# Linear attention and a switched feed-forward on one core: first expert weights behind batch 1, gate weights cast later, paired copies grouped by bank

## The chip, the cores and the metric

The kernel runs on one core of a Trainium2 chip. The metric is the device time of one execution in microseconds (us). Before the change three runs gave 202.13, 200.18 and 201.58 us; the median is 201.58.

## The reference

```python
q_s = softmax(q, axis=-1)            # over the 64 elements of a head
k_s = softmax(k, axis=2)             # over the 576 positions
kv  = einsum('bhsd,bhse->bhde', k_s, v)
x   = (q_s @ kv) -> rows (8*576, 8*64) = (4608, 512)
logits = x @ w_gate + modality_bias[modality_id]
e = argmax(logits); gate = softmax(logits)[e]
out[row] = gate * (relu(x[row] @ w1[e]) @ w2[e])
```

There are 8 batches, 8 heads, 576 positions, 64 elements a head, 8 experts of 512 x 1024 x 512. Everything comes and goes as float32.

## The kernel before, in words

A row's modality is one of two, and its bias makes one expert likely for all rows of that modality. So the kernel finds two experts, A and B, from the bias alone, loads only their weights, and sorts the rows by modality: rows of A fill the buffer `xs` from the left, rows of B from the right. At the end it counts the rows whose true argmax is the assumed expert, checks that each pass read rows that were already in place, and repeats the work for all experts if a check fails (this does not happen with these inputs).

**Attention, batch by batch (0 to 7).** SyncE (SP) loads q, k and v; batches 0 and 1 come in two halves each of 576 KB, later ones whole. ScalarE takes exp of q in place (line 855) and of k into `ek` (888); a cast of v into `vb` (898) is on ScalarE for batches 0 and 1 and on GpSimd or ScalarE later. VectorE sums q (861), inverts (872, 873), and the normalised q goes to `eq` (877): on VectorE for batches 0 to 2, on GpSimd after. TensorE forms k^T v (990, two times 18 matmuls, one for each half of the heads), VectorE scales it into a block-diagonal `kvbd` (1017 to 1026). TensorE sorts q by a permutation matrix `perm` (1066), which is evicted to `et` (1078, 1080), and multiplies by `kvbd` (1105). Each result bank holds two chunks of 64 rows, and each chunk is copied twice into `xs` (1136), to side A and to side B at an offset read from a register (1040). In batches 0 and 1 ScalarE makes the copies of side A and VectorE those of side B; later batches have one engine for both.

**Feed-forward.** Side A and side B have nine passes of 256 rows each, and one more block of 128 rows in the middle has a path of its own. A pass is 16 matmuls for its two logits (1174; 8 for each 128 rows), 32 of 256 columns with W1 (1241), evictions `hT` (1208, 1210), and 16 of 512 columns with W2 (1254), scaled by the gate (1214, 1216) and scattered by GpSimd (1219).

**Order.** Nothing is scheduled at run time. A planner (class `Plan`) gets for each step the engines it may run on with assumed durations, a rank, what it depends on, and the buffers it takes; it plays the program through and writes the instructions in the order of its start times, each engine in one fixed queue. Where the planner sees TensorE idle before a time `quiet` it puts in matmuls that nobody reads (1498). The order of the transfers is the list `transfers` (line 391): numbers are batches, "a1" is the first weight matrix of expert A, "a2" its second, likewise for B. SP issues the batches; GpSimd issues the weights, which are cast on the way (534, 545). `w_awaits` holds a weight issue until the first tensor of the batch ahead of it has landed, and `ahead_of` holds a batch until the weights ahead of it have.

```python
transfers = [0, "a1", 1, "a2", 2, "b1", "b2", *range(3, B)]
l_wg = pl.op({"DMA": (0.4, 3.5)}, load_wg, rank=0)
wg_c = pl.op(
    on_dve(32), lambda _: nc.vector.tensor_copy(out=wg_sb, in_=wg_f), [l_wg, c_dve2], rank=11
)
```

The gate weights `wg_f` (466) are loaded behind batch 0 and cast to bf16 (526).

Of the kernel before, what the change touches and what calls it, by code (L numbers as in the profile page):

```python
# [15 lines left out]
ALU = mybir.AluOpType  # L16
ACT = mybir.ActivationFunctionType
# [202 lines left out]
def on_act(n):  # L220
    return {"ACT": (0.065 + n / 1200, 0.27 + n / 1200)}


def on_dve(n, rate=1, port=False):
    return {"DVE": (0.065 + n / 960 / rate, 0.28 + n / 960 / rate, port)}
# [17 lines left out]
def kernel(  # L243
# [12 lines left out]
    nc = tc.nc  # L256
    B, H, S, Dh = q.shape
# [5 lines left out]
    NJ = S // 64  # L263
# [21 lines left out]
    pl = Plan()  # L285
# [102 lines left out]

    issued = {}

    transfers = [0, "a1", 1, "a2", 2, "b1", "b2", *range(3, B)]

    ahead_of, w_awaits = {}, {}
    for i, x in enumerate(transfers):
# [82 lines left out]
    ahead = next(i for i, x in enumerate(transfers) if isinstance(x, str))  # L477
    for b in transfers[:ahead]:
        load_batch(b)
    l_wg = pl.op({"DMA": (0.4, 3.5)}, load_wg, rank=0)  # L480


    key = sb([P, 2], FP32, "key")
# [24 lines left out]
    def experts(_):  # L508
# [16 lines left out]
    wg_c = pl.op(  # L525
        on_dve(32), lambda _: nc.vector.tensor_copy(out=wg_sb, in_=wg_f), [l_wg, c_dve2], rank=11
    )
# [299 lines left out]
    final, edge, scaled_q = [], {}, []  # L827
# [7 lines left out]
        )  # L835

    started = {"a": False, "b": False}
    filled, perms = {}, []

    copier = [("ACT", "DVE")] * 2 + [(e, e) for e in ("DVE", "ACT", "ACT", "DVE", "ACT", "ACT")]  # L840

    def attention(b):
# [3 lines left out]
        R = 10.0 * b  # L846
# [79 lines left out]
        for (h, n), e in zip(halves, eqx):  # L926
# [5 lines left out]
                    rank=R + 1,  # L932
# [4 lines left out]
        for h, n in halves:  # L937
# [5 lines left out]
                    rank=R + 2,  # L943
# [5 lines left out]
        nq = []  # L949
        for j0, n in groups:  # L950
            n_ = n * HG * Dh
            ncost = on_pool(n_, 1.88)
            if b <= 2:
                ncost = on_dve(n_, 1, True)
            nq.append(
                pl.op(
                    ncost,
                    norm_q(j0, n),
                    [iq] + nq[:1],
                    rank=R + 1,  # L960
                    takes=[] if nq else [eqb],
                    uses=[eqb, qib, bq] if nq else [qib, bq],
                )
            )
# [7 lines left out]
        cv = []  # L972
        for hp in range(2):
# [5 lines left out]
                    rank=R + 0.5,  # L979
# [21 lines left out]
        for hp in range(2):  # L1001
# [5 lines left out]
                    rank=R + 2,  # L1007
# [25 lines left out]
        o_ki = pl.op({"DVE": (0.45, 0.55)}, kinv_run, kvo, rank=R + 2, takes=[kib], uses=kvp)  # L1033
        o_kb = pl.op({"DVE": (1.24, 1.4)}, kvbd_run, [o_ki, c_pool2], rank=R + 2, takes=[kvb], uses=[*kvp, kib])

        ets, win, firsts = [], [], []
        av = {}

        def load_off(e):
# [8 lines left out]

        los = [
            pl.op(  # L1050
                {e: (1.2 if e == "ACT" else 0.6, 1.3)},
                load_off,
                [o_off] + filled.get(b - 2, [])[-2:],
                rank=R + (2.2 if b == 1 else 0.2),
            )
            for e in dict.fromkeys(copier[b])
        ]
        for gi, (j0, nj) in enumerate(groups):
            sbuf = Buf(r_ps)
            w = nj * 64  # L1060

            def s1(_, j0=j0, nj=nj, sbuf=sbuf):
                t = ps_t[sbuf.idx]
                for jj in range(nj):
                    for hp in range(2):
                        nc.tensor.matmul(  # L1066
                            out=view(t, [[2 * nj * 64, 2], [1, 64]], hp * nj * 64 + jj * 64),
                            lhsT=eq[eqb.idx][:, j0 + jj, P * hp : P * hp + P],
                            rhs=perm[pmb.idx][:, j0 + jj, :],
                            start=True,  # L1070
                            stop=True,
                        )

            def ev(e, j0=j0, nj=nj, sbuf=sbuf):
                dst = view(et[etb.idx], [[S, KD], [1, nj * 64]], j0 * 64)
                src = view(ps_t[sbuf.idx], [[nj * 64, KD], [1, nj * 64]])
                if e == "ACT":
                    nc.scalar.copy(out=dst, in_=src)  # L1078
                else:
                    nc.vector.tensor_copy(out=dst, in_=src)  # L1080

            o1 = pl.op(
                on_pe(*[P] * (2 * nj)),
                s1,
                [nq[gi], o_pm] + firsts,
                rank=R + 3,
                takes=[sbuf] if gi else [sbuf, etb],
                uses=[eqb, pmb],
                lag=lag,
            )  # L1090
            firsts = firsts or [o1]
            o2 = pl.op(
                {**on_act(KD * w), **on_dve(KD * w)},
                ev,
                [o1],
                rank=R + 3,
                uses=[sbuf, etb],
            )
            ets.append(o2)
        for gi, (j0, nj) in enumerate(groups):  # L1100
            xbuf = Buf(r_ps)

            def s2(_, j0=j0, nj=nj, xbuf=xbuf):
                for c in range(KD):
                    nc.tensor.matmul(  # L1105
                        out=view(ps_t[xbuf.idx], [[1, nj * 64]], c * nj * 64),
                        lhsT=kvbd[kvb.idx][:, c, :],
                        rhs=et[etb.idx][:, c, j0 * 64 : (j0 + nj) * 64],
                        start=True,
                        stop=True,  # L1110
                    )

            o3 = pl.op(
                on_pe(*[nj * 64] * KD),
                s2,
                [ets[gi], o_kb],
                rank=R + 4,
                takes=[xbuf],
                uses=[kvb, etb],
                lag=lag,  # L1120
            )
            for jj in range(nj):
                for side in range(2):

                    def put(e, jj=jj, j0=j0, nj=nj, side=side, xbuf=xbuf):
                        c = b * NJ + j0 + jj
                        a = av[e][(j0 + jj) // 2]
                        if j0 + jj < NJ - 1:
                            a = a >> 16 if jj else a & 0xFFFF
                        a = nc.s_assert_within(a, 0, 64 * c, skip_runtime_bounds_check_because=WHY)  # L1130
                        if side:
                            a = a + (N - 64 - 64 * c)
                        p = next(x for x in (passes_b if side else passes_a) if x[0] >= b)
                        dst = window(a, p, 64)
                        src = view(ps_t[xbuf.idx], [[nj * 64, KD], [1, 64]], jj * 64)
                        w_ = nc.scalar.copy(out=dst, in_=src) if e == "ACT" else nc.vector.tensor_copy(out=dst, in_=src)  # L1136
                        if b >= 3 and not started["ab"[side]]:
                            started["ab"[side]] = True
                            for before in id_ins:
                                sync(w_, before, "windows overlap the digits of places")  # L1140
                        if not j0 + jj and b:
                            sync(w_, edge[side], "windows of the batch before reach into this one's")
                        if j0 + jj == NJ - 1:
                            edge[side] = w_
                        if b == B - 1:
                            final.append(w_)

                    before = win[-2] if len(win) > 1 else filled[b - 1][side - 2] if b else None

                    across = win[-1 - 2 * side] if j0 + jj == NJ - 1 else None  # L1150
                    same = before and before.costs.keys() == {copier[b][side]}
                    win.append(
                        pl.op(
                            on_dve(256) if copier[b][side] == "DVE" else on_act(256),
                            put,
                            [o3, o_id if b >= 3 else None, *los, None if same else before, across],
                            rank=R + 4,
                            uses=[xbuf],
                        )
                    )  # L1160
                    if same:
                        pl.follow(win[-1], before)
        filled[b] = win


    L = sb([P, NSL, E], FP32, "L")
# [324 lines left out]
        gs = [ffn(side, *p, rank=2.0 * i + side) for side, p in enumerate((pa, pb))]  # L1491
    ffn_rest(gs, 2.0 * i + 0.7)

    quiet = 32.0

    def unread(_):

# [11 lines left out]
    cnt = sb([P, 1], FP32, "cnt")  # L1509
# [22 lines left out]
    for i, (n, need) in enumerate(early):  # L1532
        so_far = aoff[0:1, NJ * (n + 1) : NJ * (n + 1) + 1]
        o_ = 1 + 2 * i
        nc.vector.tensor_scalar(
            out=ok[:, o_ : o_ + 1], in0=so_far, scalar1=float(need), scalar2=None, op0=ALU.is_ge
        )
        nc.vector.tensor_scalar(
            out=ok[:, o_ + 1 : o_ + 2],
            in0=so_far,  # L1540
            scalar1=float(S * (n + 1) - need),
            scalar2=None,
            op0=ALU.is_le,
        )
    okm = sb([1, 1], FP32, "okm")
    nc.vector.tensor_reduce(out=okm, in_=ok, op=ALU.min, axis=AX.X)
    nrest = sb([1, 1], I32, "nrest")
# [108 lines left out]
```

## Time and profile before

| what | value |
|---|---|
| runs | 202.13, 200.18, 201.58 us |
| profiled execution | 200.07 us, span 198.4 us |
| TensorE busy | 181.1 us, 91% of the span |
| VectorE / ScalarE / GpSimd busy | 152.3 / 124.5 / 94.8 us |
| granted TensorE clock, mean | 0.987 |
| unread matmuls of line 1498 | 57, 15.3 us |

The profiled execution's 200.07 us are its span and 1.67 us around it. Spans of TensorE are modelled where matmuls are pipelined, so a busy TensorE is not one at its peak; a clock of 1.00 is 2.4 GHz, 0.50 is 1.2 GHz.

### The profile page before, as it was taken

How to read it: one execution, taken by the hardware profiler on the slowest of the kernel's cores; microseconds unless marked ns; L12 is line 12 of the kernel's file. 1: busy time of each engine (PE TensorE's matmuls, PEld its weight loads, DVE VectorE, ACT ScalarE, POOL GpSimd, SP SyncE). 2: the span in 40 equal slices, each digit the busy share in tenths (PEclk: the TensorE clock that was granted, in tenths of full speed). 3: DMA queues.
4: the chain of work that ended last, by engine and by line, in shares of the span. 5: the costliest groups of instructions: out<-in, count | busy, mean ns of one | idle time of the engine just before them, and what ended most of it. 6: DMA issues, size and time to landing. Idle time of an engine off the chain costs nothing.

```text
span 198.4 us, 5000 instructions
## 1 busy us (share of the span) xinstructions
PE 181.1 (91%) x1757; PEld 123.9 (62%) x1757; DVE 152.3 (77%) x406; ACT 124.5 (63%) x246; POOL 94.8 (48%) x119
## 2 busy tenths in 40 slices
PE   0979986789999999999999999999899999999970
PEld 0435474457596666758685867586757756766740
DVE  3879998789999997958878999856788656655750
ACT  2765889679494786999998996699898000000000
POOL 7089303944540369598496329893112311331241
PEclk9999999699999999999999999999999999999998
DMA  5999999999999999998979941120202102211202
GB/s 189 355 280 259 390 294 247 397 287 211 212 336 407 399 389 340 295 377 267 386 288 280 398 165 55 56 109 0 109 0 107 76 33 106 106 56 53 96 32 90
DMA packets 18588, 42.33 MB, mean 213 GB/s; under 512 B 1913, under 2 KB 1913, under 8 KB 18562
## 3 DMA queue, kind: packets, MB, share of 16 engines
q1 hardware_dynamic: 13344, 28.33, 40.2%
q0 software_dynamic: 5200, 13.64, 23.8%
q8 instruction: 14, 0.23, 0.4%
q14 instruction: 12, 0.10, 0.1%
q10 hardware_dynamic: 18, 0.04, 0.1%
HBM read 36.75 MB, written 9.70 MB: 234 GB/s over the span
## 4 chain that ended last, share of the span: by engine, by line
PE 58%; DVE 17%; ACT 8%; issue 4%; DMA 4%; SPq 3%; POOL 2%; DVEq 1%; ACTq 0%
PE ps L1254 24%; PE ps L1241 23%; DVE xs L1136 5%; ACT xs L1136 4%; DMA wg_f<-in_moe_w_gate_dram 4%; PE ps L990 3%; DVE eq L877 3%; DVE xs L713 3%; PE ps L1105 2%; PE ps L1066 2%; SPq L414 2%; DVE kvbd L1026 2%; PE ps L1174 2%; DVE own L861 1%; POOL eq L877 1%
## 5 line engine op out<-in xcount | busy, mean ns | idle before, releaser
L1241 PE MATMUL ps<-xs,W 128*128 128x256 bf16 x576 | 68.3, 273 | 0.0
L1254 PE MATMUL ps<-W,hT 128*128 128x512 bf16 (+1 forms) x296 | 67.2, 378 | 0.0
L1219 POOL DMA_INDIRECT out_dram<-y_sb,idx x36 | 36.1, 1002 | 59.1 <-DVE y_sb L1216 31.8
L1241 PEld LDWEIGHTS <-W 128*128 128x128 bf16 x576 | 54.9, 98 | 8.4
L1254 PEld LDWEIGHTS <-hT 128*128 128x128 bf16 x296 | 28.5, 99 | 29.1 <-issue 1.4
L1136 ACT CAST xs<-ps 128x256 f32 (+1 forms) x90 | 29.7, 430 | 6.2 <-DVE xs L1136 3.8
L1210 DVE TENSOR_SCALAR hT<-ps 128x512 bf16<-128x512 f32 x41 | 27.9, 689 | 7.1 <-PE ps L1241 5.6
L1216 DVE TENSOR_SCALAR y_sb<-ps,gate 128x512 f32<-128x512 f32 (+1 forms) x26 | 18.9, 729 | 18.3 <-PE ps L1254 13.9
L877 POOL TENSOR_TENSOR eq<-st,qi 128x512 bf16<-128x512 f32 (+1 forms) x25 | 23.8, 979 | 5.6 <-ACT xs L1136 2.9
L861 DVE TENSOR_REDUCE own<-st 128x18 f32<-128x1152 f32 x16 | 21.7, 1354 | 0.7 <-ACT st L855 0.4
L1136 DVE CAST xs<-ps 128x256 f32 (+1 forms) x54 | 19.9, 419 | 2.9 <-ACT xs L1136 1.9
L1208 ACT ACTIVATE hT<-ps 128x512 bf16<-128x512 f32 x33 | 19.1, 604 | 4.0 <-PE ps L1241 2.8
L1078 ACT CAST et<-ps 128x512 bf16<-128x512 f32 (+1 forms) x32 | 16.1, 552 | 6.1 <-PE ps L1066 6.1
L855 ACT ACTIVATE st<-st 128x1152 f32<-128x1152 f32 x16 | 18.4, 1165 | 2.3 <-DMA st<-in_q_dram 2.3
L888 ACT ACTIVATE ek<-st 128x1152 bf16<-128x1152 f32 x16 | 18.5, 1168 | 1.7 <-DMA st<-in_k_dram 1.3
L898 POOL CAST vb<-st 128x1152 bf16<-128x1152 f32 x10 | 11.2, 1145 | 11.4 <-DMA st<-in_v_dram 10.9
L1498 PE MATMUL ps<-ones 128*128 128x512 bf16 x57 | 15.3, 407 | 0.0
L1066 PE MATMUL ps<-perm,eq 128*128 128x128 bf16 x144 | 12.7, 220 | 0.2 <-POOL eq L877 0.2
L990 PE MATMUL ps<-vb,ek 64*128 64x129 bf16 x288 | 11.0, 217 | 1.9 <-ACT vb L898 1.8
L990 PEld LDWEIGHTS <-ek 64*128 64x128 bf16 x288 | 8.3, 93 | 7.0 <-ACT vb L898 2.8
L1105 PE MATMUL ps<-et,kvbd 128*128 128x128 bf16 (+1 forms) x160 | 10.8, 221 | 1.7 <-DVE kvbd L1026 1.7
L1105 PEld LDWEIGHTS <-kvbd 128*128 128x128 bf16 x160 | 9.9, 102 | 3.3 <-DVE kvbd L1026 2.0
(134 smaller groups left out, 170.8 us busy)
## 6 DMA issues: line engine op xcount, KB each, us to landing
st<-in_q_dram SPq DMA_DIRECT2D x6, 1152.0 KB, 7.7
st<-in_k_dram SPq DMA_DIRECT2D x6, 1152.0 KB, 9.8
st<-in_v_dram SPq DMA_DIRECT2D x6, 1152.0 KB, 12.4
st<-in_q_dram SPq DMA_DIRECT2D x4, 576.0 KB, 5.1
st<-in_k_dram SPq DMA_DIRECT2D x4, 576.0 KB, 7.0
st<-in_v_dram SPq DMA_DIRECT2D x4, 576.0 KB, 9.6
W<-in_moe_w_dram POOLq DMA_DIRECT2D x8, 256.0 KB, 6.6
W<-in_moe_w_dram POOLq DMA_DIRECT2D x4, 512.0 KB, 10.6
```

The costliest lines, as they stand in the source:

```text
L861: nc.vector.tensor_reduce(out=sums[qib.idx][:, h * NJ : (h + n) * NJ], in_=view(st[bq.idx], [[Dh, n * NJ], [1, Dh]], h * NJ * Dh), op=ALU.add,
L877: (nc.vector if e == "DVE" else nc.gpsimd).tensor_tensor(out=view(eq[eqb.idx], [[HG * Dh, n], [Dh, HG], [1, Dh]], j0 * HG * Dh), in0=view( ...
L888: nc.scalar.activation(out=view(ek[ekb.idx], [[Dh, n], [HG * Dh, NJ], [1, Dh]], h * Dh), in_=view(st[bk.idx], [[NJ * Dh, n], [Dh, NJ], [1, ...
L990: nc.tensor.matmul(out=ps_t[kvp[hg].idx][:, 130 * hp : 130 * hp + 129], lhsT=ek[ekb.idx][rows, j, P * hp : P * hp + P], rhs=vb[vbb.idx][ro ...
L1105: nc.tensor.matmul(out=view(ps_t[xbuf.idx], [[1, nj * 64]], c * nj * 64), lhsT=kvbd[kvb.idx][:, c, :], rhs=et[etb.idx][:, c, j0 * 64 : (j0 ...
L1136: w_ = nc.scalar.copy(out=dst, in_=src) if e == "ACT" else nc.vector.tensor_copy(out=dst, in_=src)
L1208: nc.scalar.activation(out=dst, in_=src, func=ACT.Relu)
L1210: nc.vector.tensor_scalar_max(out=dst, in0=src, scalar1=0.0)
L1216: nc.vector.tensor_scalar(out=dst, in0=src, scalar1=g, scalar2=None, op0=ALU.mult)
L1219: s_ = nc.gpsimd.indirect_dma_start(out=out, out_offset=bass.IndirectOffsetOnAxis(ap=ix[:, c : c + 1], axis=0), in_=ysb, in_offset=None, b ...
L1241: m = nc.tensor.matmul(out=t[:, i * w : (i + 1) * w], lhsT=w1(W[:, slot_, :], kd, f), rhs=xs[:, kd, lo : lo + w], start=(kd == 0), stop=(k ...
L1254: nc.tensor.matmul(out=t, lhsT=h[:, kf, i * P : (i + 1) * P], rhs=W[:, slot_, W2 + kf * D + c0 : W2 + kf * D + c0 + cn], start=(kf == 0), ...
```

## The change

Seven edits. (1) "a1" moves behind batch 1 in the list of transfers; the loading of the gate weights stays behind batch 0. (2) The cast of the gate weights follows the last normalising step of batch 0. (3) The normalised q of batch 1 goes to GpSimd. (4) In batches 0 and 1 the copies of side B of a bank follow both copies of side A of that bank; the tie between the two sides at a batch's last chunk stays in the last batch alone. (5) Register loads and one permutation matrix get later places by new dependences. (6) `quiet` is 40 where it was 32. (7) The 16 small comparisons of the side counts take an operand that exists only at the end, so they cannot stand earlier.

```diff
-    transfers = [0, "a1", 1, "a2", 2, "b1", "b2", *range(3, B)]
+    transfers = [0, 1, "a1", "a2", 2, "b1", "b2", *range(3, B)]
     for b in transfers[:ahead]:
         load_batch(b)
-    l_wg = pl.op({"DMA": (0.4, 3.5)}, load_wg, rank=0)
+        if not b:
+            l_wg = pl.op({"DMA": (0.4, 3.5)}, load_wg, rank=0)
...
+    def copy_cost(engines, side):
+        apart = engines[0] != engines[1]
+        if engines[side] == "DVE":
+            return {"DVE": (0.46, 0.65)} if apart else on_dve(256)
+        return {"ACT": (0.4, 0.55)} if apart else on_act(256)
...
-            if b <= 2:
+            if b in (0, 2):
                 ncost = on_dve(n_, 1, True)
...
+        kvbds.append(o_kb)
...
-                {e: (1.2 if e == "ACT" else 0.6, 1.3)},
+                {e: (1.2 if e == "ACT" else 0.85, 1.3)},
                 load_off,
                 [o_off] + filled.get(b - 2, [])[-2:],
-                rank=R + (2.2 if b == 1 else 0.2),
+                rank=R + (2.2 if b < 2 else 0.2),
...
+        if not b:
+            for o in los:
+                pl.later(o, nq[-1] if "DVE" in o.costs else cv[-1])
...
-                    across = win[-1 - 2 * side] if j0 + jj == NJ - 1 else None
+                    across = win[-1 - 2 * side] if j0 + jj == NJ - 1 and b == B - 1 else None
...
-                            on_dve(256) if copier[b][side] == "DVE" else on_act(256),
+                            copy_cost(copier[b], side),
...
+            if copier[b][0] != copier[b][1]:
+                for o in win[-2 * nj + 1 :: 2]:
+                    pl.later(o, win[-2])
         filled[b] = win
+        if not b:
+            pl.later(wg_c, scaled_q[0])
+        if b == 1:
+            pl.later(perms[1], kvbds[0])
+            for o in los:
+                pl.later(o, filled[0][-1])
...
-    quiet = 32.0
+    quiet = 40.0
...
+        for at, bound, op in ((o_, need, ALU.is_ge), (o_ + 1, S * (n + 1) - need, ALU.is_le)):
+            nc.vector.scalar_tensor_tensor(
+                out=ok[:, at : at + 1],
+                in0=so_far,
+                scalar=float(bound),
+                in1=cnt[0:1, 0:1],
+                op0=op,
+                op1=ALU.mult,
+            )
```

VectorE between the inverted sums of batch 0 (`qi`) and its `kvbd`, before (`ok` are the comparisons of the side counts):

```order
L873 RECIPROCAL qi_86<-qi_86 128x36
L526 CAST wg_sb<-wg_f 128x32
L1535 TENSOR_SCALAR ok<-aoff 1x1
L877 TENSOR_TENSOR eq_70<-st_63,qi_86 128x512 x4
L877 TENSOR_TENSOR eq_70<-st_63,qi_86 128x256
L1017 TENSOR_SCALAR kinv_88<-ps_93 128x2
L1017 TENSOR_SCALAR kinv_88<-ps_94 128x2
```

The same place with the change (line numbers are those of the changed file; 885 was 877, 527 was 526, 1049 was 1040):

```order
L881 RECIPROCAL qi_86<-qi_86 128x36
L885 TENSOR_TENSOR eq_70<-st_63,qi_86 128x512 x4
L885 TENSOR_TENSOR eq_70<-st_63,qi_86 128x256
L1025 TENSOR_SCALAR kinv_88<-ps_93 128x2
L1025 TENSOR_SCALAR kinv_88<-ps_94 128x2
L1028 RECIPROCAL kinv_88<-kinv_88 128x4
L1049 TENSOR_LOAD offp
L1034 TENSOR_TENSOR kvbd_74<-ps_93,kinv_88 64x2x64 x2
L1034 TENSOR_TENSOR kvbd_74<-ps_94,kinv_88 64x2x64 x2
L527 CAST wg_sb<-wg_f 128x32
```

The cast of the gate weights went from ahead of the five normalising steps to behind `kvbd`, and the comparisons are gone from here.

ScalarE around the end of batch 0's copies, before (`st_66` is q of batch 1, `ek_69` and `vb_73` its k and v, `hT` the first pass's evictions):

```order
L1136 COPY xs<-ps_95 128x4x64
L855 ACTIVATE st_66<-st_66 128x1152
L1136 ISA
L1136 COPY xs<-ps_93 128x4x64
L855 ACTIVATE st_66<-st_66 128x1152
L888 ACTIVATE ek_69<-st_67 128x2x9x64
L1208 ACTIVATE hT_80<-ps_91 128x2x256
L888 ACTIVATE ek_69<-st_67 128x2x9x64
L1208 ACTIVATE hT_80<-ps_92 128x2x256
L1208 ACTIVATE hT_80<-ps_95 128x2x256
L898 CAST vb_73<-st_64 128x2x9x64
```

With the change (863 was 855, 1148 was 1136, 906 was 898, 896 was 888, 1230 was 1208); both steps on q of batch 1 now stand ahead of batch 0's copies, behind the evictions of `et`:

```order
L1148 COPY xs<-ps_95 128x4x64
L1148 ISA
L1148 COPY xs<-ps_93 128x4x64
L906 CAST vb_73<-st_64 128x2x9x64
L896 ACTIVATE ek_69<-st_67 128x2x9x64
L906 CAST vb_73<-st_64 128x2x9x64
L896 ACTIVATE ek_69<-st_67 128x2x9x64
L1049 TENSOR_LOAD offp
L1230 ACTIVATE hT_80<-ps_95 128x2x256
```

The first pass's evictions moved behind all of batch 1's k and v. On TensorE the same holds: the first 32 matmuls with W1 stood ahead of batch 1's k^T v (line 990); now they stand behind it, in pieces of 16, 8 and 8 among batch 1's sorting matmuls (1066), and the two halves of the first W2 product stand among and behind batch 1's line 1105.

GpSimd from the first weight issues on, before (a `DMA W` of 64x2x1024 is half of a W1 part, one of 128x2x1024 half of W2):

```order
L534 DMA W<-in_moe_w_dram 64x2x1024
L679 TENSOR_TENSOR slot<-na,kt 128x72
L680 TENSOR_TENSOR slot<-slot,pos 128x72
L681 TENSOR_TENSOR slot<-slot,aoff 128x72
L684 COPY slot_141<-slot 64x36 x2
L703 TENSOR_SCALAR isb<-place,aoff 128x36
L704 TENSOR_TENSOR bsel<-isb,biasd 128x288
L707 TENSOR_TENSOR bsel<-bsel,bias_b 128x288
L708 TENSOR_SCALAR krow<-isb,keyd,key 128x36
L545 ISA
L545 DMA W<-in_moe_w_dram 128x2x1024
```

With the change:

```order
L546 DMA W<-in_moe_w_dram 128x2x1024
L680 TENSOR_TENSOR slot<-na,kt 128x72
L681 TENSOR_TENSOR slot<-slot,pos 128x72
L682 TENSOR_TENSOR slot<-slot,aoff 128x72
L685 COPY slot_141<-slot 64x36 x2
L704 TENSOR_SCALAR isb<-place,aoff 128x36
L705 TENSOR_TENSOR bsel<-isb,biasd 128x288
L708 TENSOR_TENSOR bsel<-bsel,bias_b 128x288
L709 TENSOR_SCALAR krow<-isb,keyd,key 128x36
L885 TENSOR_TENSOR eq_71<-st_66,qi_87 128x512 x4
L885 TENSOR_TENSOR eq_71<-st_66,qi_87 128x256
```

The issue of W2 moved up to right behind that of W1, ahead of `slot` and `bsel`, and the five normalising steps of batch 1 were added behind them.

## Rows read from the trace of the kernel before

**Rows 1.** Windows of the span: busy us (instructions) by engine, granted clock, DMA share, GB/s.

```profile
12.00:18.00 6.00, 5.05 (x62) 2.71 (x62) 4.72 (x14) 3.67 (x5) 5.55 (x9) 1.00 1.11 196
...
30.00:36.00 6.00, 3.52 (x59) 2.33 (x57) 5.24 (x16) 6.00 (x13) 3.16 (x4) 1.00 1.00 284
36.00:42.00 6.00, 5.99 (x34) 3.25 (x34) 3.80 (x12) 3.64 (x10) 5.91 (x9) 0.72 1.05 386
...
60.00:80.00 20.00, 19.55 (x192) 13.13 (x189) 18.33 (x47) 14.36 (x21) 9.78 (x10) 1.00 1.04 384
```

**Rows 2.** The chain of work that ended last: start us, us, what.

```profile
32.02 1.05 ACT vb L898
33.12 0.72 PE ps L990 x18
...
77.55 1.73 PE ps L1254 x8
79.28 0.56 PE ps L1066 x10
...
81.56 1.01 PE ps L1105 x20
...
91.50 3.49 PE ps L1241 x32
```

**Rows 3.** Timeline, batch 0: start us, us, engine line operation [idle before <- what ended it].

```profile
10.21 1.16 ACT L888 ACTIVATE ek<-st 128x1152 bf16<-128x1152 f32 x1 [0.31 <-DMA st<-in_k_dram]
...
11.71 1.15 ACT L898 CAST vb<-st 128x1152 bf16<-128x1152 f32 x1 [0.34 <-DMA st<-in_v_dram]
...
13.31 0.36 DVE L873 RECIPROCAL qi<-qi 128x36 f32<-128x36 f32 x1
...
13.96 1.16 ACT L898 CAST vb<-st 128x1152 bf16<-128x1152 f32 x1 [1.09 <-DMA st<-in_v_dram]
...
14.96 0.22 DVE L526 CAST wg_sb<-wg_f 128x32 bf16<-128x32 f32 x1 [1.28 <-DMA wg_f<-in_moe_w_gate_dram]
...
15.16 2.81 DVE L877 TENSOR_TENSOR eq<-st,qi 128x512 bf16<-128x512 f32 x5
...
16.32 2.67 ACT L1078 CAST et<-ps 128x512 bf16<-128x512 f32 x5 [1.20 <-PE ps L1066]
```

**Rows 4.** Windows of 1 us while W2 of A was issued and moved.

```profile
23.00:24.00 1.00, 1.00 (x6) 0.48 (x5) 0.83 (x3) 1.00 (x2) 1.00 (x2) 1.00 1.05 410
...
28.00:29.00 1.00, 1.00 (x12) 0.90 (x10) 0.93 (x4) 1.00 (x2) 0.00 (x0) 1.00 1.15 228
```

**Rows 5.** Timeline, GpSimd around the weight issues.

```profile
10.38 2.67 POOL L534 DMA_DIRECT2D W<-in_moe_w_dram  x4 [5.82 <-DVE pos L648]
...
13.03 0.38 POOL L679 TENSOR_TENSOR slot<-na,kt 128x72 f32<-128x72 f32 x1
...
19.37 0.36 POOL L708 TENSOR_SCALAR krow<-isb,keyd,key 128x36 f32<-128x36 f32 x1
...
22.86 1.53 POOL L545 DMA_DIRECT2D W<-in_moe_w_dram  x2 [3.12 <-DMA st<-in_q_dram]
```

**Rows 6.** Timeline, GpSimd at batch 2's v.

```profile
46.71 2.24 POOL L898 CAST vb<-st 128x1152 bf16<-128x1152 f32 x2 [4.80 <-DMA st<-in_v_dram]
```

**Rows 7.** Timeline, copies into xs in batch 0 and then batch 1.

```profile
20.08 3.22 ACT L1136 CAST xs<-ps 128x256 bf16<-128x256 f32 x8 [1.10 <-PE ps L1105]
...
36.79 0.43 DVE L1136 CAST xs<-ps 128x256 f32 x1 [0.17 <-ACT xs L1136]
```

**Rows 8.** Timeline, TensorE from the second pass on.

```profile
42.74 0.26 PEld L1174 LDWEIGHTS <-xs 128*128 128x128 bf16 x8 [1.04 <-DVE xs L1136]
...
48.41 1.89 PE L1254 MATMUL ps<-W,hT 128*128 128x512 bf16 x8
...
50.24 0.69 PE L990 MATMUL ps<-vb,ek 64*128 64x129 bf16 x18
```

**Rows 9.** The page, costliest groups: busy, mean ns of one, idle before.

```profile
L877 POOL TENSOR_TENSOR eq<-st,qi 128x512 bf16<-128x512 f32 (+1 forms) x25 | 23.8, 979 | 5.6 <-ACT xs L1136 2.9
```

More of the change, by code (lines that the diff above doesn't have):

```diff
@@ L837 @@
     started = {"a": False, "b": False}
-    filled, perms = {}, []
+    filled, perms, kvbds = {}, [], []
+    def copy_cost(engines, side):
[3 more added lines that the diff above has]
+        return {"ACT": (0.4, 0.55)} if apart else on_act(256)
     copier = [("ACT", "DVE")] * 2 + [(e, e) for e in ("DVE", "ACT", "ACT", "DVE", "ACT", "ACT")]
@@ L1534 @@
         o_ = 1 + 2 * i
[L1535 to L1544, printed above, removed]
+        for at, bound, op in ((o_, need, ALU.is_ge), (o_ + 1, S * (n + 1) - need, ALU.is_le)):
[7 more added lines that the diff above has]
+            )
     okm = sb([1, 1], FP32, "okm")
```

## The prediction, made before the changed kernel ran

> **What bounds the kernel now.** I read the windows of the span first. Between 60 and 80 us TensorE is busy 19.55 of 20 us at a granted clock of 1.00, and the DMA engines are full as well (share 1.04, 384 GB/s) [rows 1]. From 30 to 36 us TensorE works 3.52 of 6 us [rows 1]. So there are two stages: a start, in which TensorE waits for loads and for the attention of batches 0 and 1, and a long saturated part. The chain of waits says the same: at 32.02 it leaves ScalarE's cast of v of batch 1, goes through the k^T v of line 990, and is later W1, W2, sorting and attention matmuls on TensorE, of which one piece of each kind is shown [rows 2]. The time is therefore "when TensorE becomes saturated with a given amount of work left" plus a fixed rest. What the change touches all lies in the start, apart from the 16 small comparisons at the end.
>
> My marks for the start are on TensorE: the second pass's logits at 42.74, its last W2 product at 48.41, and k^T v of batch 2 at 50.24 [rows 8]. Up to there both orders do the same useful work: attention of two batches, both logits, two passes with W1, two with W2. If the change reaches these marks x us earlier and the rest stays saturated, the kernel is x us shorter.
>
> **Batch 0.** VectorE inverts q's sums at 13.31 for 0.36 us, then waits 1.28 us for the load of the gate weights, casts them, and only at 15.16 starts `eq` [rows 3]. Now `eq` follows at 13.31 + 0.36 = 13.7, 1.5 us earlier. The evictions `et` began 16.32 - 15.16 = 1.16 us after `eq` and took 2.67 [rows 3]: now 14.9 to 17.5. On ScalarE come then two exp of q of batch 1 and later two steps on k and two on v; each is a pass over 128x1152 at the 1.05 of the chain's `vb` [rows 2]. q: 17.5 + 2.1 = 19.6. Nine copies of batch 0 to side A, 3.22 / 8 = 0.40 each [rows 7]: 23.2. Four more passes for k and v: 27.4. One k^T v at 0.72 [rows 2] overlaps the last pass only in part: batch 1's k^T v is over at about 28.2, against 33.12 + 0.72 = 33.8.
>
> **The loads for that.** k and v halves of batch 0 came 11.71 - 10.21 = 1.5 us apart, each 576 KB [rows 3]. The last half of v came at 13.96 beside W1's bytes [rows 3]; without them 11.71 + 1.5 = 13.2, and the gate weights by about 14.2 (I give them at most 1 us). Six halves at 1.5 follow: q 17.2, k 20.2, v 23.2 if nothing shares the engines. Before, q was there at 22.86 only, as the release of the W2 issue shows [rows 5]. So loads don't hold up the sum above: ScalarE wants v between 23 and 26.
>
> **W1 of A, the new wait.** It was issued at 10.38 [rows 5]; now GpSimd issues it when q of batch 1 has landed, 17.2. The issue takes 2.67 and that of W2, now right behind, 1.53 [rows 5]. When the bytes move is the unknown. Before, W2 of A was in the same position, issued at 22.86 with k and v still on their way: at 23 to 24 the engines moved 410 GB/s, and at 28 to 29 only 228 [rows 4]. I read the high rate as loads and the low one as weights that are cast on the way, so the weights came mostly after the loads; in the stretch with W1 the mean was 196 GB/s [rows 1]. W1 is 512 x 1024 numbers, 2.1 MB to read at 410 GB/s, 5.1 us, or 1.05 MB to write as bf16 at 196 GB/s, 5.3 us. Then it lands at 23.2 + 5.3 = 28.5, and its matmuls start at about 28.8. That is 0.6 us behind batch 1's k^T v: a tie, with W1 just last.
>
> From 28.8 TensorE has left, before the second logits: 32 matmuls of W1 3.49, 18 for sorting at 0.056 = 1.0, 20 of line 1105 at 1.01, two W2 halves at 1.73 each [rows 2], and 7 unread ones at 15.3 / 57 = 0.27 (from the table), of which I count 1.5 and the rest in waits. Sum 10.5; logits at 39.3, with some waiting for banks 39.7. That is **3.0 us earlier** than 42.74 [rows 8]. The copies of batch 1 must be there too: before, VectorE and ScalarE passed the turn back and forth (VectorE's idle time at 36.79 ended by ScalarE's copy [rows 7]); now each runs through its own, 9 x 0.40 on ScalarE and 9 x 0.43 on VectorE, beside each other, 3.9 us from about 35.5. Also a tie, at 39.4.
>
> **GpSimd.** Its `slot` to `krow` block took 13.03 to 19.73 [rows 5], 6.7 us. Now it starts when both weights are issued: 17.2 + 2.67 + 1.53 + 6.7 = 28.1. The normalised q of batch 1 comes behind it, 4.5 full pieces at 0.98 [rows 9] = 4.4, so done at 32.5. TensorE's sorting of batch 1 stands between the W1 pieces and needs the last about 33.9. Slack 1.4; I cost this at nothing. If GpSimd were 2 us later it would cost 0.6.
>
> **From the logits on.** Between logits and the next mark lie 48.41 - 42.74 = 5.67 us of work [rows 8]: 45.4, and k^T v of batch 2 would be due at 47.1. But its v landed at 46.71, where GpSimd's cast waited 4.80 us for it; two casts took 2.24 [rows 6], so the first half is ready at 46.71 + 1.1 = 47.85. The DMA engines are full up to there, 1.05 from 36 to 42 [rows 1], and the same bytes are ahead of it, so I leave its landing where it is. That gives 50.24 - 47.85 = **2.4 us**.
>
> **The small edits.** Register loads and the permutation matrix: they stand where engines wait anyway, 0. The comparisons: 16 on VectorE of the smallest size; in the saturated part VectorE has 20 - 13.13 us free in 20 [rows 1], and at the end they depend on what was ready long before. 0, at most 0.5 if they stand after the last copy. `quiet` 40 adds unread matmuls only where TensorE waits.
>
> **Sum.** Between 2.4 and 3.0 I take 2.6: 200.07 - 2.6 = 197.5 for the profiled execution. That execution lies 1.5 us under the median of the runs, 201.58; against the median it is **199.0**. About 1%, 2.0 us, is what a measurement of this kernel can tell from no change.
>
> **Rivals.**
> - *W1 and v of batch 1 share the engines (0.17).* If the weights get half from 17.2 + 1 on, v lands near 27.4 in place of 23.2 (the bytes of v beside as many of W at about 230 GB/s), the two casts and k^T v end at 30.2, W1's matmuls start behind them at 30.3: 1.5 later than 28.8, so the gain is 1.4 and the time 200.2. For it: the windows with both show 196 GB/s [rows 1]. Against it: the second of 410 GB/s with W2 issued [rows 4]. The Trainium skill, "DMA: Bandwidth & Descriptors", section "Queues, rings and completion order", says that each DMA engine goes round robin between the queues it has work for, a packet at a time; by that rule this rival is the forecast, and the windows at 23 to 24 us speak against a plain half-and-half.
> - *The clock falls over the first W1 pass (0.13).* Before, the granted clock was 0.72 from 36 to 42, right after a stretch with TensorE busy 3.52 of 6 [rows 1]; there it cost little, since W1 ran while copies were awaited. Now TensorE idles in a like way between batch 0's attention and 28.8. At half clock the 3.49 us of W1 and a part of the sorting take twice as long, of which 1.3 is seen: 200.3. The larger `quiet` fills part of this gap with unread work, which is the argument against.
> - *v starves (0.06), slower.* GpSimd now issues W1 and W2 of A together at 17.2, while k and v of batch 1 are on their way. If weights go first, 11 us of them stand ahead of the rest of v: it lands at about 34, k^T v ends at 36.9, and with the 10.9 us between k^T v and the logits of the forecast (all of it stands behind k^T v in TensorE's order) they come at 47.8, 5.1 late: 206.7. It decides as soon as v still misses bytes when the first weights flow. Before, loads kept 410 GB/s with W2 issued [rows 4], so little.
> - *Nothing comes of it (0.14).* The full DMA engines from 36 us on [rows 1] hold batches 3 and later and B's weights to their old times, and what is won is lost again there: 201.6. Against it: TensorE, not a load, ended most steps of the chain behind 50 us [rows 2].
>
> **Chances and range.** The forecast has 0.50. Faster by over 1%: most of the forecast (0.43), a little of the first two rivals (0.07): 0.50. Within 1%: 0.07 of the forecast, 0.22 of the first two rivals, 0.12 of the last: 0.41. Slower: starving and mishaps of the last: 0.09. The range: low end, 3.0 us, the 1.04 that TensorE waited for copies ahead of the logits [rows 8] if that goes as well, and 1.1 by which runs stand off their median, 196.4; high end, the last rival's 201.6 and a little for measurement, 202.0. It leaves out the starving and part of the tails.
>
> **What would show it.** `eq` of batch 0 at 13.7 on VectorE; W1 issued near 17.2 and its first matmuls at 28.8, released by the weights; cast of the last half of v of batch 1 started before 27; granted clock 1.00 from 28 to 40; second logits near 39.7; k^T v of batch 2 near 47.9, released by v's cast; and behind it the same saturated stretch. If W1's matmuls wait for v's k^T v past 30, the first rival holds; a clock of 0.5 there is the second; v cast after 30 the third; and if the marks come 2.5 us earlier and the end does not, the fourth. I would be wrong above all in the landing times of W1 and v, the only numbers with no row of their own.

## The result, and the profile after

Twenty runs of each kernel gave a median of 199.11 us (197.70 to 203.47) for the changed one and 201.09 us (199.71 to 202.97) for the one before. The ratio is 0.990, with a 95% interval of 0.9876 to 0.9925. Ratios here and below leave out disturbed executions, over 1.5% above the fastest of the same kernel (3 of 20 of the changed kernel, 7 of 12 with `quiet` at 32, 8 of 18 with W1 first), so they need not be the ratio of two medians, and three traces of such executions (`quiet` at 32, the first series with W1 first, copies on two engines in all batches) are not compared in time. The profiled execution took 197.98 us, its span 196.4; before it was 200.07 and 198.4. Forecast were 199.0 and, for the profiled execution, 197.5. The forecast took its 2.6 us from 201.58, the median of three runs; the median of the twenty is 201.09, so the gain measured is 2.0 us.

Windows of the changed kernel, columns as in [rows 1]:

```profile
12.00:18.00 6.00, 6.00 (x72) 3.46 (x71) 5.05 (x12) 4.18 (x8) 1.24 (x2) 1.00 1.07 378
...
30.00:36.00 6.00, 6.00 (x61) 4.51 (x59) 5.73 (x21) 5.81 (x16) 6.00 (x8) 1.00 0.93 265
36.00:42.00 6.00, 6.00 (x62) 4.12 (x60) 5.50 (x14) 5.84 (x12) 6.00 (x10) 1.00 1.04 377
...
60.00:80.00 20.00, 19.73 (x191) 13.13 (x189) 18.62 (x44) 15.48 (x26) 12.02 (x13) 1.00 1.04 395
```

Between 12 and 18 us the loads now move 378 GB/s, where the rate was 196 while W1 moved. From 30 to 42 us TensorE is busy throughout, in part with unread matmuls, at a clock of 1.00, where it had a hole and then a clock of 0.72.

Timeline of the changed kernel, the rows that answer to [rows 3, 5, 6, 7, 8], in order of time:

```profile
13.69 2.83 DVE L885 TENSOR_TENSOR eq<-st,qi 128x512 bf16<-128x512 f32 x5
...
16.75 2.67 POOL L535 DMA_DIRECT2D W<-in_moe_w_dram  x4 [12.19 <-DVE kinv L1025]
...
18.96 0.18 DVE L527 CAST wg_sb<-wg_f 128x32 bf16<-128x32 f32 x1
...
20.00 3.65 ACT L1148 CAST xs<-ps 128x256 bf16<-128x256 f32 x9
...
26.71 1.16 ACT L896 ACTIVATE ek<-st 128x1152 bf16<-128x1152 f32 x1
...
28.77 1.91 PE L1263 MATMUL ps<-xs,W 128*128 128x256 bf16 x16
...
29.02 4.69 POOL L885 TENSOR_TENSOR eq<-st,qi 128x512 bf16<-128x512 f32 x5 [3.94 <-issue]
...
39.42 0.34 PE L1196 MATMUL ps<-wg_sb,xs 128*128 128x8 bf16 x8
...
45.23 2.25 POOL L906 CAST vb<-st 128x1152 bf16<-128x1152 f32 x2 [2.35 <-DMA st<-in_v_dram]
...
46.43 0.69 PE L998 MATMUL ps<-vb,ek 64*128 64x129 bf16 x18
```

`eq` starts at 13.69, ScalarE makes nine copies in a row and is through with batch 1's k at 27.87, W1's matmuls start at 28.77 without having waited, the second logits come at 39.42 (42.74 before), and k^T v of batch 2 at 46.43, **3.8 us earlier** than 50.24 [rows 8]. But the end is only 2.0 us earlier. What lies between is in the view of TensorE's waits, which gives who waited, for whom, us in total, how often and the longest. Of the kernel before, from its k^T v of batch 2 to the end:

```profile
PE ps L1174 <- ACT xs L1136: 0.7, 1, 0.7
PE ps L1174 <- DVE xs L1136: 0.5, 1, 0.5
PE ps L1066 <- POOL eq L877: 0.2, 1, 0.2
```

and of the changed kernel:

```profile
PE ps L1196 <- ACT xs L1148: 0.9, 1, 0.9
PE ps L1078 <- POOL eq L885: 0.7, 1, 0.7
PE ps L1263 <- ACT hT L1230: 0.6, 1, 0.6
PE ps L1196 <- DVE xs L1148: 0.3, 1, 0.3
PE ps L1078 <- ACT et L1090: 0.2, 1, 0.2
```

TensorE waited 1.3 us in this stretch before and waits 2.8 now. In these two traces that is 1.5 of the 1.8 us that were given back. But these are the waits of one execution. Two of the kernels below, without unread matmuls and with other copies of the last batch, have every engine's useful work up to 115 us in the order of the changed kernel. TensorE's timelines of the changed kernel and of these two, at the same 32 matmuls:

```profile
107.35 3.68 PE L1263 MATMUL ps<-xs,W 128*128 128x256 bf16 x32
...
107.90 3.68 PE L1263 MATMUL ps<-xs,W 128*128 128x256 bf16 x32
...
106.02 3.68 PE L1263 MATMUL ps<-xs,W 128*128 128x256 bf16 x32
```

From k^T v of batch 2 (46.43, 48.32, 46.44) that is 60.92, 59.58 and 59.58 us. So the changed kernel's profiled execution lost 1.3 us here that two other executions of this order did not lose, most of it between 50 and 56 us. There ScalarE began the third pass's `hT` late. First the changed kernel, then the one with other last copies:

```profile
53.34 1.57 ACT L1230 ACTIVATE hT<-ps 128x512 bf16<-128x512 f32 x3 [2.70 <-PE ps L1078]
...
50.65 0.59 ACT L1230 ACTIVATE hT<-ps 128x512 bf16<-128x512 f32 x1
```

Why it did is open.

### The profile page after: what moved, and what is told of

It is laid out like the page before. It is cut to its first block, busy times and chain, and to the rows that moved or that the text cites. A ratio compares the mean times of both kernels' runs of the same rounds, so it can differ in the third digit from the quotient of the medians.

```text
span 196.4 us, 5025 instructions
## 1 busy us (share of the span) xinstructions
PE 182.7 (93%) x1771; PEld 125.0 (64%) x1771; DVE 150.7 (77%) x403; ACT 122.4 (62%) x243; POOL 97.9 (50%) x125
## 4 chain that ended last, share of the span: by engine, by line
PE 68%; ACT 8%; DMA 8%; DVE 6%; issue 4%; POOL 2%; ACTq 1%; DVEq 0%; POOLq 0%
PE ps L1276 25%; PE ps L1263 23%; DMA st<-in_v_dram 6%; PE ps L1520 6%; ACT xs L1148 5%; PE ps L998 4%; PE ps L1078 3%; PE ps L1117 2%; DVE xs L1148 2%; DMA mraw<-in_moe_modality_id_dram 1%; PE ps L1196 1%; ACT ek L896 1%; DVE kvbd L1034 1%; DVE eq L885 1%; PE ps L1419 1%
## 5 line engine op out<-in xcount | busy, mean ns | idle before, releaser
L1232 DVE TENSOR_SCALAR hT<-ps 128x512 bf16<-128x512 f32 x43 | 29.4, 687 | 6.3 <-PE ps L1263 3.9
L885 POOL TENSOR_TENSOR eq<-st,qi 128x512 bf16<-128x512 f32 (+1 forms) x30 | 28.4, 976 | 6.7 <-issue 4.1
L1238 DVE TENSOR_SCALAR y_sb<-ps,gate 128x512 f32<-128x512 f32 (+1 forms) x22 | 16.0, 726 | 17.6 <-PE ps L1276 12.9
L1230 ACT ACTIVATE hT<-ps 128x512 bf16<-128x512 f32 x31 | 18.2, 626 | 7.1 <-PE ps L1263 4.3
L1520 PE MATMUL ps<-ones 128*128 128x512 bf16 x71 | 20.4, 424 | 0.0
L1090 ACT CAST et<-ps 128x512 bf16<-128x512 f32 (+1 forms) x28 | 15.1, 579 | 4.3 <-PE ps L1078 4.1
L906 POOL CAST vb<-st 128x1152 bf16<-128x1152 f32 x11 | 12.4, 1150 | 7.7 <-PE ps L998 5.4
L1236 ACT ACTIVATE y_sb<-ps,gate 128x512 f32<-128x512 f32 x15 | 10.3, 695 | 7.2 <-PE ps L1276 5.9
L1078 PEld LDWEIGHTS <-eq 128*128 128x128 bf16 x144 | 9.9, 98 | 4.4 <-POOL eq L885 1.2
L1520 PEld LDWEIGHTS <-ones 128*128 128x128 bf16 x71 | 7.0, 107 | 8.2 <-issue 3.3
```

Of the source, the lines that this page charges most:

```text
L885: (nc.vector if e == "DVE" else nc.gpsimd).tensor_tensor(out=view(eq[eqb.idx], [[HG * Dh, n], [Dh, HG], [1, Dh]], j0 * HG * Dh), in0=view( ...
L1078: nc.tensor.matmul(out=view(t, [[2 * nj * 64, 2], [1, 64]], hp * nj * 64 + jj * 64), lhsT=eq[eqb.idx][:, j0 + jj, P * hp : P * hp + P], rh ...
L1230: nc.scalar.activation(out=dst, in_=src, func=ACT.Relu)
L1232: nc.vector.tensor_scalar_max(out=dst, in0=src, scalar1=0.0)
L1520: nc.tensor.matmul(out=ps_t[n_ps - 1], lhsT=ones, rhs=view(ones, [[0, 4], [1, P]]), start=True, stop=True)
```

## The experiments

Each kernel was timed in five rounds beside the kernel before; the ratios are to the kernel before.

### The list alone

```
-    transfers = [0, "a1", 1, "a2", 2, "b1", "b2", *range(3, B)]
+    transfers = [0, 1, "a1", "a2", 2, "b1", "b2", *range(3, B)]
```

> The kernel before with nothing but the list of transfers changed (W1 of A behind batch 1). Theory (the place of W1 carries the gain alone): k^T v of batch 2 at 47 or before, ratio 0.99. Rival (the other edits are needed to use the earlier loads: VectorE normalises batch 1 between its copies, the two sides still wait for each other): k^T v of batch 2 at 48 to 50, ratio 0.995 to 1.00.

Measured: 1.027 (1.0213 to 1.0329), slower. Neither theory had this. Since the gate weights' load stands behind all batches that are ahead of the first weights, moving W1 alone moves that load behind batch 1. Timelines of TensorE and VectorE:

```profile
29.44 0.55 PE L1174 MATMUL ps<-wg_sb,xs 128*128 128x8 bf16 x16 [4.24 <-DVE wg_sb L526]
...
29.20 0.18 DVE L526 CAST wg_sb<-wg_f 128x32 bf16<-128x32 f32 x1 [3.05 <-DMA wg_f<-in_moe_w_gate_dram]
```

The first logits wait 4.24 us for 32 columns of gate weights. The transfers by queue from 22 to 25 us (packets, MB, share of 16 engines; q1 are SP's loads, q0 GpSimd's weights):

```profile
q0 software_dynamic: 323, 0.58, 104.3%
q1 hardware_dynamic: 168, 0.05, 14.5%
```

The small load moves beside the weights, 168 of its packets in 3 us.

### The list, with the gate weights' load kept behind batch 0

```
-    l_wg = pl.op({"DMA": (0.4, 3.5)}, load_wg, rank=0)
+        if not b:
+            l_wg = pl.op({"DMA": (0.4, 3.5)}, load_wg, rank=0)
```

> The kernel before with the list of transfers changed and the load of the gate weights kept behind batch 0, as in the change, and nothing else. In the run with the list alone the gate weights stood behind batch 1 and landed between 25 and 29 us among W1's packets; TensorE waited 4.24 us for their cast ahead of its first logits. Theory (that wait is what made the list alone slower, and the earlier batch 1 is worth what the prediction says): first logits at 24 to 26, k^T v of batch 2 at 46 to 48, ratio 0.985 to 0.995. Rival (the freed start needs the copies by bank and GpSimd's normalising as well): first logits early, k^T v of batch 2 at 49 to 51, ratio 0.997 to 1.01.

Measured: 0.9986 (0.9954 to 1.0018), the rival. TensorE's timeline:

```profile
25.22 0.81 PE L1175 MATMUL ps<-wg_sb,xs 128*128 128x8 bf16 x16 [0.97 <-DVE xs L1137]
...
42.27 0.83 PE L1175 MATMUL ps<-wg_sb,xs 128*128 128x8 bf16 x16 [2.06 <-DVE xs L1137]
...
51.03 0.69 PE L991 MATMUL ps<-vb,ek 64*128 64x129 bf16 x18
```

The wait for gate weights is gone and with it the loss, but the earlier batch 1 isn't worth anything yet: the second logits wait 2.06 us for VectorE's copies, and k^T v of batch 2 is at 51.03, as late as before.

### The same, with batch 1 normalised on GpSimd

```
-            if b <= 2:
+            if b in (0, 2):
```

> The kernel before with three lines changed: the list of transfers, the gate weights' load behind batch 0, and the normalised q of batch 1 on GpSimd. List and gate load alone left the time at 0.9954 to 1.0018 of before; TensorE waited 2.06 us for VectorE's copies ahead of the second logits. Theory (VectorE is what the earlier batch 1 then waits for, so GpSimd's normalising is the edit that lets the gain through): logits of the second pass before 41, ratio 0.985 to 0.993. Rival (the copies of the two sides still wait for each other, and that is the limit): second logits at 42 or later, ratio 0.995 to 1.00.

Measured: 0.9895 (0.984 to 0.9949), as fast as the whole change.

```profile
41.39 0.56 PE L1175 MATMUL ps<-wg_sb,xs 128*128 128x8 bf16 x16 [1.06 <-ACT xs L1137]
...
48.40 0.69 PE L991 MATMUL ps<-vb,ek 64*128 64x129 bf16 x18
```

The wait ahead of the second logits is halved, and ended by ScalarE now; the logits are 0.9 us earlier, less than the theory named (before 41), k^T v of batch 2 is 2.6 us earlier.

### The change without GpSimd's normalising

The diff above, undone on the changed kernel.

> The changed kernel with the normalised q of batch 1 on VectorE again. Theory (VectorE's 2.8 us for it stand in the way of the copies and of kvbd now that q comes earlier): k^T v of batch 2 or the second pass's logits 1 to 3 us later, ratio 0.995 to 1.005. Rival (it has slack on either engine): marks within 0.5 us, ratio 0.99.

Measured: 0.9902 (0.9865 to 0.994). The marks did move as the theory had it, the time did not:

```profile
32.20 0.40 PE L1078 MATMUL ps<-perm,eq 128*128 128x128 bf16 x4 [0.20 <-DVE eq L885]
...
41.49 0.34 PE L1196 MATMUL ps<-wg_sb,xs 128*128 128x8 bf16 x8
...
48.93 0.69 PE L998 MATMUL ps<-vb,ek 64*128 64x129 bf16 x18
```

k^T v of batch 2 is 2.5 us later than in the changed kernel and the end no later. With the copies by bank the normalising may stay on VectorE.

### The change without the copies by bank

```
-            if copier[b][0] != copier[b][1]:
-                for o in win[-2 * nj + 1 :: 2]:
-                    pl.later(o, win[-2])
...
-                            copy_cost(copier[b], side),
+                            on_dve(256) if copier[b][side] == "DVE" else on_act(256),
```

> The changed kernel with the copies of batches 0 and 1 in the old order, one to side A and one to side B in turn. Theory of the prediction (copies that no longer wait for the other side let ScalarE get to k and v of batch 1 sooner): first pass with W1 1 to 2 us later than 28.8, second logits 1 to 2.5 us later, ratio 0.993 to 1.00. Rival (ScalarE has slack there): marks within 0.5 us, ratio 0.99.

(The tie between the sides at a batch's end came back as well.) Measured: 0.9977 (0.9938 to 1.0017): the gain is gone, as the theory had it. The first pass with W1 starts at 31.33, 2.6 us later, which is more than the theory's 1 to 2.

```profile
31.33 1.04 PE L1259 MATMUL ps<-xs,W 128*128 128x256 bf16 x8
...
49.68 0.68 PE L998 MATMUL ps<-vb,ek 64*128 64x129 bf16 x18
```

### W1 ahead of batch 1 again

The change of the list alone, undone on the changed kernel, in two series.

> The changed kernel with W1 of A back ahead of batch 1 in the list of transfers, everything else as changed. Theory (the place of W1 sets the start): batch 1's q lands 4 to 5 us later again, its k^T v ends near 32 instead of 28.6, k^T v of batch 2 comes at 49 to 50 instead of 46.4, and the time goes back to the one before: ratio to before 0.997 to 1.003. Rival (the gain is that of GpSimd's normalising and of the copies): the mark stays within 1 us of 46.4 and the ratio at 0.99.

> The changed kernel with W1 of A ahead of batch 1 once more, since the first series left 0.983 to 0.997. Theory (the place of W1 sets the start): ratio 0.995 to 1.00, k^T v of batch 2 at 49 or later. Rival (W1's place is worth nothing by itself once the rest is changed): ratio 0.988 to 0.992.

Measured: 0.9897 (0.9828 to 0.9966) and 0.9931 (0.9889 to 0.9973). Of the second run, TensorE:

```profile
23.85 1.91 PE L1263 MATMUL ps<-xs,W 128*128 128x256 bf16 x16
...
30.40 0.68 PE L998 MATMUL ps<-vb,ek 64*128 64x129 bf16 x18 [1.62 <-ACT vb L906]
...
42.60 0.35 PE L1196 MATMUL ps<-wg_sb,xs 128*128 128x8 bf16 x8 [2.18 <-ACT xs L1148]
```

The place of W1 does set the start, as the theory said: W1 runs 5 us earlier, batch 1's k^T v 4.6 us later and the second logits 3.2 us later. But the time doesn't follow: it falls short of the changed kernel by less than the intervals tell apart, and it is faster than before. So both theories were half right, and no run shows that the place of W1 is worth time by itself.

### quiet at 32

> The changed kernel with quiet at 32 again. Theory of the prediction (quiet only adds unread matmuls where TensorE waits): same marks to 50 us, ratio 0.99. Rival (quiet is also the time at which the planner may give the eighth bank of results to other work, so the order of everything behind 32 us is another one): k^T v of batch 2 still within 0.5 us of 46.4, but other waits of TensorE behind it, and a ratio up to 1.00.

One number, undone. Measured: 0.9888 (0.9848 to 0.9928), no difference from the changed kernel. The order is another, as the rival had it: of the second pass's W1 matmuls 8 stand between its two halves of logits, where the changed kernel has 16. It costs nothing that can be measured.

### No unread matmuls from 18 us on

```
-        for o in pl.fill(pl.order({r_ps: (quiet, n_ps - 1)}), 4.5, quiet, 0.3, 0.216, 10, Op({"PE": (0.216, 0.45)}, unread)):
+        for o in pl.fill(pl.order({r_ps: (quiet, n_ps - 1)}), 4.5, 18.0, 0.3, 0.216, 10, Op({"PE": (0.216, 0.45)}, unread)):
```

> The changed kernel in the same order, without the unread matmuls that the plan has behind 18 us (some 45 of 71 gone). Theory of the clock: TensorE does little between 20 and 28.7 us, the granted clock goes to 0.50 in some stretch between 24 and 36, the first pass and the sorting take up to 1.7 us longer and the second logits come up to 1.7 us later: ratio 0.993 to 1.00. Rival (the clock stays, or falls where TensorE waits anyway): marks within 0.5 us, ratio 0.99.

Measured: 0.9948 (0.9911 to 0.9984), in the range of the theory of the clock, though the interval still touches that of the changed kernel (0.9876 to 0.9925). The trace decides. Windows:

```profile
18.00:24.00 6.00, 1.55 (x27) 1.27 (x28) 4.71 (x11) 5.75 (x13) 5.47 (x13) 0.92 1.10 306
24.00:30.00 6.00, 3.69 (x56) 2.81 (x54) 4.83 (x12) 3.97 (x4) 1.97 (x3) 0.50 1.11 209
30.00:36.00 6.00, 6.00 (x54) 5.01 (x53) 4.60 (x20) 3.88 (x11) 6.00 (x8) 0.73 0.90 269
```

and the timeline of TensorE:

```profile
29.11 3.60 PE L1263 MATMUL ps<-xs,W 128*128 128x256 bf16 x16
```

After a window with TensorE busy 1.55 of 6 us the clock is 0.50, 1.2 GHz, and it is still there when W1 starts: the first 16 matmuls take 3.60 us in place of 1.91. k^T v of batch 2 comes at 48.32, 1.9 us late.

### Other copies of the last batch

```
-    copier = [("ACT", "DVE")] * 2 + [(e, e) for e in ("DVE", "ACT", "ACT", "DVE", "ACT", "ACT")]
+    copier = [("ACT", "DVE")] * 2 + [(e, e) for e in ("DVE", "ACT", "ACT", "DVE", "ACT")] + [("ACT", "DVE")]
```

> The changed kernel with the last batch's copies on two engines, side A on ScalarE and side B on VectorE, as in batches 0 and 1 (before: all 18 on ScalarE). Theory (part of the 3.8 us that the changed kernel is ahead at batch 2 is given back at the end of the attention, where TensorE waits 0.93 us for ScalarE's copies): that wait goes, all else stays up to 125 us, 0.9 to 1.9 us shorter than the changed kernel, ratio 0.981 to 0.986. Rival (VectorE is behind with hT, y_sb and kvbd of the last batch, and the wait moves there): ratio 0.99 or above.

Measured: 0.9865 (0.9809 to 0.992), the profiled span 194.2. The ratio is just outside the theory's range, and the interval reaches the rival's. In the changed kernel TensorE has run out of work when ScalarE finishes the last batch (timeline):

```profile
137.75 4.01 ACT L1148 CAST xs<-ps 128x256 f32 x10 [0.73 <-DVE y_sb L1238]
...
141.82 0.95 PE L1196 MATMUL ps<-wg_sb,xs 128*128 128x8 bf16 x32 [0.93 <-ACT xs L1148]
```

With two engines at these copies that wait is gone (TensorE's waits from 46 us on):

```profile
PE ps L1078 <- POOL eq L885: 0.9, 1, 0.9
PE ps L1078 <- DVE hT L1232: 0.2, 1, 0.2
```

Of the 2.2 us between the spans this edit has about 1.0: the changed kernel's trace was 1.3 us behind already at 107 us, where both orders are the same (rows above).

The same edit on the kernel before:

> The kernel before with the last batch's copies on two engines, side A on ScalarE and side B on VectorE. On the changed kernel the same edit took the profiled span from 196.4 to 194.2 us. Theory (the changed kernel reaches batch 2 3.8 us earlier and so runs into the end of the attention, which is limited by ScalarE's copies; before, TensorE itself was late there): the gain is smaller here, 0 to 0.7 us, ratio 0.996 to 1.00. Rival (the copies of the last batch bind in the same way whatever comes before): 2 us, ratio 0.990.

Measured: 1.008 (1.0047 to 1.0114), slower by 0.8%, which neither theory had; both started from the whole 2.2 us as the edit's. Timelines of ScalarE, VectorE and TensorE:

```profile
141.57 0.37 ACT L1136 CAST xs<-ps 128x256 f32 x1 [1.03 <-DVE xs L1136]
...
145.04 1.41 DVE L1136 CAST xs<-ps 128x256 f32 x3 [0.65 <-ACT xs L1136]
...
147.11 0.60 PE L1254 MATMUL ps<-W,hT 128*128 128x512 bf16 x2 [1.40 <-DVE hT L1210]
```

Without the copies by bank the two engines wait for each other, VectorE's `hT` stands behind that, and TensorE waits 1.40 us for it. So this run doesn't tell whether the end of the attention would have bound before; that stays open.

Copies on two engines in all batches (the same pair eight times in that line):

> The changed kernel with the copies of all batches on two engines, side A on ScalarE and side B on VectorE. Theory (behind 50 us TensorE waits for copies and for GpSimd's eq in spots, since one engine has 18 copies of a batch in a row): the waits go, another 0.5 to 1.5 us below the run with the last batch alone, ratio 0.975 to 0.985. Rival (copies of two engines are slower one by one, 0.43 against 0.29 to 0.35 us, and take turns, which costs what they bring): ratio 0.985 to 0.995.

Measured: 0.9855 (0.9809 to 0.9902), the lowest ratio, and not apart from that with the last batch alone; the interval reaches into both theories' ranges. That these two beat the changed kernel is not shown: the intervals overlap.

## Why the prediction was right, and where it was not

The time was right, 199.11 against 199.0, but by luck. The gain at the mark was mis-sized and its way to the end was wrong, and these two cancelled in part: 2.6 us were forecast and 2.0 measured. The rest is the base, 201.58 from three runs, which lay 0.5 us above the median of twenty.

**The start: right.** `eq` at 13.7 (13.69), W1 issued at 17.2 (16.75), its matmuls at 28.8 (28.77), second logits at 39.7 (39.42), clock 1.00. The nine copies in a row, the four passes of ScalarE and the tie between W1 and batch 1 hold to 0.5 us. That GpSimd's normalising is done in time holds too, but by less and for another reason: GpSimd stood idle for 3.94 us from 25.08 on, so its block before was over 3 us earlier than forecast, and the normalising began at 29.02, not 28.1, since its input was ready only at 28.89. It ended at 33.71; the last sorting matmuls, at 33.77 on TensorE, did not wait.

**The mark at batch 2: mis-sized.** The step that left v of batch 2 where it was was wrong: GpSimd's cast began at 45.23 in place of 46.71 and k^T v at 46.43 in place of 47.85. The gain there was 3.8, not 2.4.

**"The rest stays saturated": wrong.** That is the step that failed. The mark came 3.8 us earlier and the time fell by 2.0. A balance of the profiled executions of eleven kernels, one execution of each, shows where such a difference goes: from the start of k^T v of batch 2 to the end of the last W2 matmul, the time in which TensorE ran neither a matmul nor a weight load, and what is left.

| kernel | k^T v of batch 2 | last W2 ends | TensorE waits between | rest |
|---|---|---|---|---|
| before | 50.24 | 192.43 | 1.28 | 140.9 |
| changed | 46.43 | 190.59 | 2.76 | 141.4 |
| list alone | 54.59 | 197.41 | 3.03 | 139.8 |
| list and gate load | 51.03 | 193.05 | 1.45 | 140.6 |
| and GpSimd's normalising | 48.40 | 189.28 | 0.25 | 140.6 |
| changed, normalised on VectorE | 48.93 | 191.04 | 2.12 | 140.0 |
| changed, copies in turn | 49.68 | 192.22 | 1.70 | 140.8 |
| changed, no unread matmuls | 48.32 | 192.02 | 2.77 | 140.9 |
| changed, W1 first (second series) | 51.94 | 192.44 | 0.07 | 140.4 |
| changed, last copies on two engines | 46.44 | 188.25 | 1.06 | 140.8 |
| before, last copies on two engines | 50.77 | 193.71 | 1.86 | 141.1 |

The busy time behind the mark is nearly the same everywhere, 139.8 to 141.4. The time is the mark plus that work plus **waits**, and these run from 0.07 to 3.03. I had them at what they were. [Rows 1] shows 19.55 of 20 us as saturated; the missing half microsecond is of the size of the effects forecast here. The kernel with W1 first shows it best: 5.5 us late at the mark, and 1.9 late at the end; 2.7 of the difference are waits that it doesn't have, 1.0 is busy time. What decides how long TensorE waits there was shown at one place, the last batch's copies (about 1.0 us of span). For GpSimd's `eq` and ScalarE's `hT` it stays open, and part of it is not the order's: two executions of one order lay 1.3 us apart by 107 us.

**The edits.** I costed them together and could not have said which carried the gain. The list alone loses 2.7%, and with the gate load in its place it wins nothing; taken back from the changed kernel, the list costs nothing that the intervals show. With the list and the gate load either GpSimd's normalising alone or the copies by bank with the normalising left on VectorE reach the full gain, while normalising with the other edits but without the copies by bank does not. So the parts do not add up, and a part's worth here is the worth of one order that the planner made with it.

**The rivals.** *W1 and v sharing the engines*: transfers of the changed kernel by queue, first from 17 to 20 us, then from 22 to 23:

```profile
q1 hardware_dynamic: 535, 1.16, 103.9%
...
q0 software_dynamic: 102, 0.18, 96.8%
q1 hardware_dynamic: 23, 0.04, 14.1%
```

W1 is issued from 16.75 on, and up to 20 no packet of it moves; then it takes nearly all, and the last packets of v go among its own. ScalarE's casts of v, at 23.55 and 25.66, did not wait. So the forecast's reading of [rows 4] held up to 20 us and only roughly after that: the first six packets of W1 move between 20 and 21, and the last four of SP's loads, all of batch 1's v, only from 24 to 25:

```profile
q1 hardware_dynamic: 4, 0.01, 2.0%
```

The forecast had v landed at 23.2 and W1 behind it. That W1's matmuls still started at 28.77 is in part luck, and v's delay was hidden because ScalarE was not free for its last half before. The Trainium skill, "DMA: Bandwidth & Descriptors", section "Queues, rings and completion order", has each engine go round robin between queues with work; in the row from 22 to 23 and beside the gate weights of the list alone both queues do move, though not by equal numbers of packets (102 to 23, 323 to 168). The 3 us from 17 on agree only if W1's packets were not ready until then, which no run shows. *The clock* did not fall, and the run without unread matmuls shows what kept it up; its price was 1.9 us at the mark and 0.5% of the time, 1.0 us, against my 1.3. *v starving* did not happen. *Nothing gained*, the pull back by later loads: 1.8 of the 3.8 us at the mark did not reach the end, though no wait of TensorE in the list above is ended by a load. What takes them back in most executions stays open, since the waits listed are those of one.

## What to carry to other kernels

A late stage that is "97% busy" isn't a constant: an earlier start runs into its small waits, so look at each of them and who ends it before carrying a gain to the end. Before a wait is put down to an order, look for it in a second execution of the same order; here 1.3 us were in one trace alone. An order list that also fixes where a small transfer goes has to be read for that: here 4.24 us hung on 32 columns. And where a planner makes the order, test a part both by adding it to the old kernel and by taking it from the new one; the two answers differed here for the copies and the normalising.

## What the runs showed of the hardware

In the changed kernel no packet of the weights that GpSimd issued from 16.75 us on moved from 17 to 20 us, while SP's loads moved 535 packets. Loads that are still there when weights flow are slow: with the list alone SP's queue had 14.5% from 22 to 25 us beside the weights' 104.3%, and the gate weights were cast only at 29.20. Without unread matmuls the clock of 1.2 GHz lasted beyond the stretch of little work that preceded it: the granted clock was 0.50 from 24 to 30 us, and its mean still 0.73 from 30 to 36 us with TensorE busy 6.00 of 6.
